# New orders for every engine's queue in a fused attention and MLP kernel

## The chip, the cores and the metric

The kernel runs on one core of a Trainium2 chip. The metric is the time of one execution on the device, in microseconds (us); of several runs the median is given.

## The reference

Eight batches with eight heads each attend over 16 beacon keys, which every query sees, and 576 causal keys. Then comes an MLP without bias, whose activation is the sigmoid form of GELU. All arrays are float32; the kernel computes in float16 and accumulates in float32.

```python
B, H, S, D = 8, 8, 576, 64              # 16 beacons
k_all = concatenate([beacon_k, k], axis=2); v_all = likewise
scores = q @ k_all.T / 8                # causal mask on the 576 keys only
a = exp(scores - max); a /= a.sum(-1)
x = (a @ v_all).transpose(0, 2, 1, 3).reshape(4608, 512)
h = x @ w_in                            # 512 x 2048
out = (h * sigmoid(1.702 * h)) @ w_out  # 2048 x 512
```

## The kernel before

**Attention.** The work is cut into 16 sets `s`; a set is one batch and four of its heads. A set's q and k are loaded with a cast to float16 (`ldqk`, on POOL's DMA queue) and turned by 32x32 transposes on VectorE (`turn`). The scores of a set come in chunks of 512 columns: TensorE computes a chunk (`qk`, L447), ScalarE takes the exponential into the tile `E` (`exp`, L458). There is one PSUM tile for scores, so the next `qk` waits for the `exp` before it. GpSimd masks the blocks on the diagonal in place (`mask`, L479). From set 4 on, VectorE adds the blocks of `E` up (`zadd`, L497). TensorE multiplies ones with these sums, and `E` with the values (`av`, L534; `av5.2.1` is the ones-product of set 5, half 1; `.0` and `.1` are the value products). VectorE transposes the sums, takes reciprocals and transposes back (`z1`, `z2`, L546 to L557), then scales the products into `xT` (`norm`, L569).

**MLP.** Tokens come in groups `g`: two of 256, then eight of 512. `m1` (L593) is the first product, sixteen pieces for a group of 512, with GELU behind it on ScalarE (`gelu`, L614; for the first two groups `tanh`, L607, and a `gate` on VectorE, L626). The second product of groups 2 to 9 uses seven products of half size in place of eight (a Strassen form): VectorE makes four sums of the activations (`s`, L658; four steps i that build on each other, for each of four slices), TensorE computes product p in four pieces (`m2.g.p.slice`, L707), and VectorE joins the products into four output tiles (`join`, L723; the first is copied by ScalarE, `half`, L718). SyncE's queue stores them (L730). The four output tiles `osb` come from a pool of four buffers, in turn. `u` is a ring of four PSUM banks, shared by `av`, `m1` and `m2`: a piece that opens a new tile in it waits until an older one was read.

**The order.** Nothing is scheduled automatically. All 1489 steps are made as `Op`s in a `Plan` (L117), in a fixed order of creation; the number of a step is its place there. The table `ORDER` (L16) lists, for each engine and for the DMA queue `Q`, the numbers in the order in which they are to run. `Plan.run` (L147) walks the lists with assumed durations and with the assumed delays `LAT` between engines, which gives each step a start. It sorts all steps by it to merge the lists into one program, and picks the bank of `u` for each tile by it. An engine's own sequence is its list, whatever the assumed times are. Waits between engines come from the reads and writes of the steps, through semaphores.

Some numbers that are used below, with what they stand for:

```
PE    414 qk19     221 m2.1.1.3 (last piece of group 1)   292..320 m1.2.*   1256 qk49
      352 m2.2.6.6   433 av4.1.1   474, 477 av5.2.*   480 av5.0.0   1115 av12.1.1
      972..1002 m1.6.*   1473 m2.9.4.6   1479 m2.9.5.6   1483..1486 m2.9.3.*
ACT   417, 415 exp of qk19   222 copy of m2.1.1   1257 exp of qk49
DVE   326, 327, 328 three s that build on each other   92 memset of beacon tiles
      353 join   473 zadd   1474, 1480, 1481, 1487 the last four joins
POOL  61 beacon values of batch 1   378 keys of set 4   396, 390 values of batch 2
      1076 values of batch 6   723 keys of set 9 (after turn 462)
SP    187, 217 stores of groups 0 and 1   93..96 beacon keys of sets 8 to 15
```

Of the kernel before, what the change touches and what calls it, by code (L numbers as in the profile page):

```python
# [17 lines left out]
        76, 100, 115, 118, 120, 106, 138, 141, 143, 108, 155, 111, 152, 129, 161, 158, 122, 131, 164, 167, 134, 127,  # L18
        170, 173, 176, 145, 125, 148, 150, 177, 182, 188, 191, 227, 194, 197, 232, 183, 203, 234, 200, 178, 237,
        179, 206, 258, 241, 209, 184, 263, 185, 212, 265, 213, 248, 246, 268, 214, 215, 401, 251, 253, 272, 218,  # L20
        404, 275, 244, 279, 219, 220, 407, 282, 284, 277, 221, 414, 320, 296, 304, 290, 302, 292, 300, 298, 312,
        308, 294, 318, 314, 310, 306, 316, 426, 435, 423, 343, 338, 339, 340, 433, 431, 438, 344, 345, 359, 349,
        341, 464, 346, 350, 351, 352, 354, 574, 355, 429, 360, 361, 577, 356, 362, 357, 372, 365, 583, 474, 477,
        373, 366, 374, 367, 605, 480, 484, 375, 482, 607, 368, 506, 502, 488, 492, 610, 490, 486, 498, 504, 500,
        508, 514, 510, 516, 494, 496, 512, 534, 593, 596, 535, 536, 539, 540, 550, 541, 542, 537, 742, 545, 546,
        547, 548, 603, 745, 551, 552, 553, 599, 601, 619, 622, 748, 555, 556, 557, 558, 561, 755, 625, 627, 629,
        562, 563, 776, 568, 564, 569, 570, 571, 779, 764, 767, 659, 637, 641, 657, 649, 651, 647, 661, 635, 631,
        653, 805, 772, 770, 774, 643, 655, 633, 639, 645, 679, 680, 815, 818, 700, 681, 682, 684, 701, 915, 690,
        685, 686, 691, 692, 702, 918, 687, 693, 695, 703, 696, 924, 821, 823, 697, 698, 706, 946, 825, 707, 713,
        708, 709, 948, 934, 937, 714, 715, 716, 827, 951, 944, 940, 942, 853, 831, 833, 855, 857, 851, 843, 835,  # L30
        837, 847, 839, 845, 829, 849, 841, 1083, 960, 963, 875, 876, 880, 877, 878, 881, 882, 1086, 968, 966, 970,
        883, 1089, 902, 909, 903, 886, 891, 1096, 887, 888, 889, 892, 893, 1117, 904, 894, 905, 896, 897, 1120, 898,
        899, 910, 911, 1105, 1108, 1146, 912, 976, 994, 996, 972, 978, 1000, 992, 982, 974, 998, 990, 984, 988, 980,
        1002, 986, 1256, 1156, 1113, 1111, 1115, 1159, 1025, 1020, 1026, 1021, 1259, 1022, 1027, 1031, 1023, 1028,
        1265, 1164, 1162, 1166, 1041, 1042, 1287, 1036, 1047, 1032, 1048, 1033, 1037, 1038, 1034, 1039, 1289, 1054,
        1055, 1049, 1056, 1043, 1044, 1050, 1292, 1057, 1198, 1172, 1168, 1178, 1184, 1180, 1194, 1170, 1174, 1176,
        1275, 1278, 1182, 1186, 1196, 1188, 1190, 1281, 1301, 1285, 1283, 1304, 1216, 1217, 1221, 1192, 1222, 1227,
        1218, 1223, 1228, 1219, 1224, 1232, 1229, 1233, 1230, 1307, 1311, 1309, 1237, 1327, 1333, 1238, 1243, 1234,
        1244, 1235, 1323, 1239, 1245, 1250, 1251, 1341, 1240, 1246, 1252, 1253, 1337, 1405, 1315, 1331, 1343, 1411,
        1335, 1321, 1403, 1431, 1313, 1325, 1407, 1419, 1317, 1423, 1425, 1319, 1339, 1421, 1409, 1329, 1361, 1413,  # L40
        1366, 1382, 1429, 1362, 1363, 1401, 1367, 1364, 1427, 1368, 1383, 1372, 1369, 1373, 1374, 1375, 1388, 1377,
        1389, 1378, 1390, 1395, 1379, 1384, 1380, 1385, 1391, 1396, 1415, 1397, 1398, 1470, 1454, 1417, 1455, 1449,
        1471, 1450, 1451, 1476, 1452, 1456, 1477, 1457, 1478, 1460, 1461, 1462, 1463, 1465, 1466, 1467, 1468, 1472,
        1479, 1473, 1483, 1484, 1485, 1486,
# [3 lines left out]
        195, 198, 233, 235, 201, 204, 238, 180, 207, 259, 210, 264, 186, 266, 269, 216, 402, 405, 408, 222, 417,  # L48
        415, 297, 291, 303, 305, 301, 299, 293, 309, 321, 295, 319, 313, 315, 311, 307, 317, 436, 439, 342, 465,
        468, 575, 578, 584, 587, 606, 608, 503, 507, 489, 491, 493, 487, 499, 505, 509, 515, 517, 495, 501, 511,  # L50
        497, 513, 611, 538, 743, 746, 749, 756, 758, 777, 780, 660, 642, 638, 652, 658, 648, 650, 636, 632, 662,
        654, 806, 644, 634, 656, 640, 646, 809, 916, 683, 919, 928, 925, 947, 949, 952, 828, 832, 854, 856, 852,
        858, 834, 838, 844, 840, 836, 846, 830, 848, 850, 842, 1084, 879, 1087, 1090, 1099, 1097, 1118, 1121, 1147,
        1150, 977, 995, 979, 997, 993, 973, 975, 983, 991, 999, 989, 1001, 981, 1003, 985, 987, 1257, 1260, 1024,
        1269, 1266, 1288, 1290, 1293, 1199, 1179, 1173, 1181, 1185, 1195, 1171, 1169, 1175, 1177, 1183, 1187, 1197,
        1189, 1191, 1193, 1220, 1328, 1334, 1324, 1342, 1316, 1332, 1344, 1406, 1412, 1338, 1336, 1404, 1432, 1314,
        1408, 1420, 1318, 1424, 1326, 1426, 1320, 1340, 1422, 1410, 1330, 1322, 1414, 1430, 1402, 1365, 1428, 1416,
        1418, 1453,
# [3 lines left out]
        123, 163, 160, 124, 224, 169, 128, 166, 172, 175, 146, 147, 126, 149, 151, 225, 226, 398, 190, 193, 196,  # L62
        199, 255, 256, 257, 202, 205, 286, 242, 411, 287, 211, 208, 243, 399, 249, 247, 400, 250, 412, 254, 252,
        273, 245, 274, 280, 276, 413, 281, 285, 283, 278, 289, 461, 288, 462, 419, 580, 420, 463, 326, 327, 328,
        421, 322, 92, 323, 324, 422, 427, 428, 424, 425, 325, 330, 334, 329, 335, 432, 336, 331, 434, 337, 332, 333,
        470, 347, 582, 353, 471, 581, 472, 430, 473, 358, 363, 475, 476, 478, 479, 481, 485, 739, 483, 369, 376,
        370, 589, 752, 740, 590, 615, 518, 753, 921, 519, 754, 526, 591, 527, 520, 528, 592, 529, 521, 741, 522,
        597, 523, 594, 530, 595, 598, 531, 802, 532, 524, 533, 616, 543, 525, 604, 549, 617, 618, 554, 600, 620,
        602, 623, 624, 621, 559, 760, 628, 761, 762, 626, 630, 565, 763, 566, 768, 572, 765, 811, 812, 766, 803,
        804, 769, 773, 771, 671, 1080, 775, 672, 813, 922, 663, 814, 664, 675, 667, 816, 673, 819, 668, 669, 817,  # L70
        923, 665, 666, 820, 674, 676, 677, 1093, 670, 688, 694, 678, 930, 822, 824, 699, 931, 826, 932, 933, 704,
        710, 938, 939, 935, 936, 717, 711, 945, 941, 943, 1081, 956, 957, 958, 871, 1082, 1094, 1095, 959, 872, 873,
        867, 859, 961, 962, 964, 965, 860, 863, 1262, 1143, 861, 874, 862, 868, 864, 967, 865, 971, 866, 969, 884,
        869, 870, 1101, 1144, 890, 1145, 1102, 895, 1103, 1104, 900, 906, 1109, 907, 1110, 913, 1106, 1107, 1152,
        1153, 1004, 1154, 1005, 1155, 1264, 1006, 1263, 1016, 1012, 1017, 1157, 1114, 1112, 1013, 1018, 1116, 1160,
        1008, 1161, 1009, 1019, 1158, 1014, 1015, 1029, 1010, 1165, 1011, 1007, 1163, 1167, 1035, 1040, 1271, 1051,
        1045, 1058, 1052, 1297, 1272, 1273, 1274, 1298, 1299, 1276, 1279, 1300, 1200, 1204, 1280, 1201, 1277, 1205,
        1282, 1302, 1206, 1286, 1284, 1208, 1305, 1209, 1202, 1303, 1210, 1212, 1203, 1306, 1207, 1213, 1225, 1231,
        1308, 1312, 1214, 1310, 1215, 1211, 1236, 1247, 1241, 1248, 1254, 1349, 1345, 1350, 1346, 1347, 1353, 1351,
        1354, 1355, 1356, 1357, 1358, 1359, 1370, 1348, 1360, 1352, 1376, 1381, 1386, 1392, 1393, 1445, 1446, 1433,  # L80
        1399, 1437, 1434, 1438, 1447, 1435, 1441, 1442, 1436, 1443, 1444, 1439, 1448, 1440, 1458, 1464, 1469, 1480,
        1474, 1481, 1487,
    ],
    "POOL": [
        8, 10, 12, 14, 16, 17, 19, 21, 23, 25, 27, 29, 31, 33, 35, 37, 39, 41, 43, 45, 47, 110, 49, 51, 113, 114,
        53, 55, 57, 59, 133, 61, 136, 137, 63, 65, 67, 69, 71, 378, 230, 231, 229, 380, 382, 384, 386, 236, 388,
# [29 lines left out]

class Plan:  # L117

    LANES = 8
    LAT = {"PE": 230, "ACT": 178, "DVE": 212, "POOL": 110, "Q": 1400, "SP": 0}

    def __init__(self, ring):
        self.ops = []
        self.ring = ring
        self.tiles = {}
        self.closers = {}
# [1004 lines left out]
```

## Time and profile before

| | us |
|---|---|
| median of 3 runs (329.2 to 330.05) | 329.88 |
| the profiled execution's own time | 328.92 |
| its span, first to last instruction | 327.2 |
| TensorE busy in the span | 314.6 |
| VectorE busy | 237.2 |
| ScalarE busy | 202.1 |
| GpSimd busy | 113.9 |

The granted clock of TensorE was 0.999 over the span. In stretches, from the trace (busy us of each engine):

| stretch, us | TensorE | VectorE | ScalarE | GpSimd |
|---|---|---|---|---|
| 0 to 30 | 22.25 | 18.30 | 17.90 | 21.60 |
| 30 to 62 | 31.66 | 26.73 | 21.83 | 19.10 |
| 62 to 101 | 38.31 | 32.23 | 29.56 | 16.27 |
| 101 to 164 | 63.00 | 55.74 | 46.89 | 26.12 |
| 164 to 213 | 49.00 | 42.57 | 35.84 | 24.29 |
| 213 to 245 | 32.00 | 20.32 | 21.87 | 4.27 |
| 245 to 285 | 40.00 | 20.75 | 16.57 | 2.28 |
| 285 to 327 | 38.38 | 20.57 | 11.62 | 0.00 |

A busy TensorE in this count is not TensorE at its peak: matmuls overlap, and a short wait between two of them can be hidden in the modelled end of the first. So the lengths of pieces are taken below from one start to the next.

### The profile page before, as it was taken

To read this page: it belongs to the slowest core of one execution; us is meant where nothing else is said; L and a number is where in the kernel's file an instruction comes from. 1 tells how busy PE (TensorE), PEld (TensorE's weight loads), DVE (VectorE), ACT (ScalarE), POOL (GpSimd) and SP (SyncE) were. 2 spreads that over 40 slices of the span, in tenths; PEclk is the share of its full clock that TensorE was granted. 3 is DMA by queue.
4 is the path that set the end of the run, shared out by engine and by line. 5 is a ranking of instruction groups with operands and counts; after the bars stand their busy time and mean duration, and the time that the engine had idled before them with its cause. 6 is when DMAs were issued, how large, how long until landed. Compare 5 with 4: busy or idle time off the path is not lost.

```text
span 327.2 us, 9966 instructions
## 1 busy us (share of the span) xinstructions
PE 314.6 (96%) x4364; PEld 214.7 (66%) x4364; DVE 237.2 (72%) x480; ACT 202.1 (62%) x236; POOL 113.9 (35%) x178
## 2 busy tenths in 40 slices
PE   6589999999999999999999999999999999999995
PEld 6467665545775477746878878547764776447884
DVE  4838798777987989977998798858558853006674
ACT  1676697678767586679666786868577212674010
POOL 8765478190419312941177019400042000000000
PEclk9999999999999999999999999999999999999999
DMA  7999999293424911792039709500120012000122
GB/s 126 159 201 211 204 186 184 37 123 107 99 72 64 190 34 34 79 198 43 7 53 178 119 4 124 154 2 3 34 98 0 2 34 83 15 0 2 65 98 97
DMA packets 58220, 28.83 MB, mean 88 GB/s; under 512 B 41280, under 2 KB 53568, under 8 KB 58176
## 3 DMA queue, kind: packets, MB, share of 16 engines
q0 software_dynamic: 47552, 18.49, 47.9%
q1 hardware_dynamic: 10560, 9.69, 9.2%
q8 instruction: 34, 0.56, 0.7%
q14 instruction: 10, 0.08, 0.1%
q10 hardware_dynamic: 64, 0.01, 0.0%
HBM read 37.22 MB, written 9.44 MB: 143 GB/s over the span
## 4 chain that ended last, share of the span: by engine, by line
PE 83%; DMA 6%; DVE 4%; POOL 3%; ACT 2%; issue 1%; ACTq 0%; POOLq 0%
PE u L593 34%; PE u L707 30%; PE u L534 9%; PE s L447 7%; PE u L638 3%; DMA w<-in_moe_w_out_dram 3%; DMA w<-in_moe_w_in_dram 3%; ACT E L458 1%; DVE sA L658 1%; DVE g L626 1%; POOL vb L378 1%; POOL w L384 0%; DVE bkn L403 0%; ACT L614 0%; DVE kT L418 0%
## 5 line engine op out<-in xcount | busy, mean ns | idle before, releaser
L593 PE MATMUL u<-xT,w 128*128 128x512 f16 (+1 forms) x704 | 130.6, 341 | 0.6 <-ACT g L614 0.5
L458 ACT ACTIVATE E<-s 128x2048 f16<-128x2048 f32 (+5 forms) x66 | 98.9, 1515 | 44.9 <-PE s L447 44.4
L614 ACT ACTIVATE g<-u 128x512 f16<-128x512 f32 x128 | 70.5, 598 | 53.7 <-PE u L593 53.2
L593 PEld LDWEIGHTS <-w 128*128 128x128 f16 x704 | 67.6, 98 | 54.3 <-issue 1.9
L479 POOL TENSOR_SCALAR_AFFINE_SELECT E<-E 128x512 f16<-128x512 f16 (+3 forms) x78 | 49.3, 665 | 110.8 <-ACT E L458 79.1
L723 DVE SCALAR_TENSOR_TENSOR osb<-u,osb 128x512 f32<-128x512 f32 x56 | 37.3, 683 | 24.5 <-PE u L707 22.5
L707 PEld LDWEIGHTS <-g 128*128 128x128 f16 x512 | 48.3, 98 | 9.3 <-issue 0.2
L707 PE MATMUL u<-w,g 128*128 128x256 f16 x384 | 50.6, 273 | 0.0
L447 PE MATMUL s<-qT,kT 32*128 32x32 f16 (+20 forms) x1376 | 34.6, 228 | 5.7 <-ACT E L458 2.8
L447 PEld LDWEIGHTS <-kT 32*128 32x128 f16 x1376 | 25.2, 92 | 22.5 <-issue 14.4
L707 PEld LDWEIGHTS <-sA 128*128 128x128 f16 x384 | 36.3, 98 | 5.3 <-issue 0.3
L707 PE MATMUL u<-tB,sA 128*128 128x256 f16 x256 | 35.1, 273 | 0.1
L658 DVE TENSOR_TENSOR sA<-g 128x512 f16<-128x512 f16 x32 | 12.9, 416 | 26.2 <-ACT g L614 26.2
L569 DVE TENSOR_TENSOR xT<-u,rz 128x352 f16<-128x352 f32 (+2 forms) x52 | 25.5, 517 | 6.5 <-PE u L534 6.3
L378 POOL DMA_DIRECT2D vb<-in_v_dram x32 | 27.4, 876 | 2.4 <-DMA qn<-in_q_dram 1.6
L534 PE MATMUL u<-E,vb 128*32 128x352 f16 (+8 forms) x928 | 27.4, 262 | 0.0
L497 DVE TENSOR_TENSOR zs<-zs,E 128x1344 f16<-128x1344 f16 (+2 forms) x36 | 22.7, 633 | 5.3 <-POOL E L479 4.4
L534 PEld LDWEIGHTS <-vb 128*32 128x32 f16 (+1 forms) x928 | 19.9, 96 | 5.5 <-issue 1.7
L418 DVE STREAM_TRANSPOSE kT<-kn 128x576 f32<-128x576 f32 x16 | 20.1, 1257 | 2.1 <-DMA kn<-in_k_dram 1.4
L418 DVE STREAM_TRANSPOSE qT<-qn 128x576 f32<-128x576 f32 x16 | 19.9, 1241 | 0.3 <-DMA qn<-in_q_dram 0.3
L546 DVE STREAM_TRANSPOSE zt<-u 128x224 f32<-128x224 f32 (+2 forms) x32 | 15.0, 470 | 5.9 <-PE u L534 5.8
L497 DVE TENSOR_TENSOR zs<-E 128x1856 f16<-128x1856 f16 x12 | 15.8, 1320 | 3.3 <-POOL E L479 3.3
(48 smaller groups left out, 252.3 us busy)
## 6 DMA issues: line engine op xcount, KB each, us to landing
out_dram<-osb SPq DMA_DIRECT2D x36, 256.0 KB, 2.4
kn<-in_k_dram POOLq DMA_DIRECT2D x16, 288.0 KB, 6.9
qn<-in_q_dram POOLq DMA_DIRECT2D x16, 288.0 KB, 6.5
vb<-in_v_dram POOLq DMA_DIRECT2D x24, 128.0 KB, 6.4
w<-in_moe_w_in_dram POOLq DMA_DIRECT2D x8, 256.0 KB, 9.4
w<-in_moe_w_out_dram POOLq DMA_DIRECT2D x4, 512.0 KB, 13.5
vb<-in_v_dram POOLq DMA_DIRECT2D x8, 112.0 KB, 5.0
vb<-in_v_dram POOLq DMA_DIRECT2D x8, 80.0 KB, 7.9
```

What stands on the lines that cost most here:

```text
L378: nc.gpsimd.dma_start(out=t[0 : hi - lo, j, h0:h1, :], in_=v[b, h0:h1, lo:hi, :].rearrange("h n d -> n h d"),)
L418: nc.vector.transpose(out=f32(dst.rearrange("p n e -> p (n e)")).rearrange("p (r t) -> p t r", t=TR), in_=f32(src[:, :]).rearrange("p (t c ...
L447: nc.tensor.matmul(sc[:, h, o : o + w], kT[s % NB2][r : r + 32, j * P : (j + 1) * P, d], qT[s % NB2][r : r + 32, a : a + w, d], start=(d = ...
L458: nc.scalar.activation(out=Es[s][:, :, c0:c1], in_=ss[i][:, :, o : o + c1 - c0], func=AFT.Exp, scale=0.125,)
L479: nc.gpsimd.affine_select(out=blk, in_=blk, compare_op=ALU.is_ge, fill=0.0, base=off + (Nb if j == 0 else 0), pattern=[[0, Q], [1, w]], ch ...
L497: nc.vector.tensor_tensor(out=t, in0=E[:, :, Z0:S] if i == 1 else t, in1=E[:, :, wcol[i] : wcol[i] + S - a], op=ALU.add,)
L534: nc.tensor.matmul(u[32 * h : 32 * h + 32, a:e], lhs, src[0:kw, h, col : col + e - a], start=first, stop=last,)
L569: nc.vector.tensor_tensor(out=xT[:, 2 * hs + x : 2 * hs + x + n, t0 : t0 + w], in0=rings[("av", s, x, half)][:, 0 : n * w].rearrange("p (n ...
L593: nc.tensor.matmul(u[:, o + a - t0 : o + e - t0], w1t[:, kp, nt * P : (nt + 1) * P], xT[:, kp, a % XR : (e - 1) % XR + 1], start=(kp == 0) ...
L614: nc.scalar.activation(out=gts[g][:, n0:n1, 0:w], in_=rings[("m1", g, n0)][:, 0 : n * w].rearrange("p (n w) -> p n w", n=n), func=AFT.Gelu ...
L707: nc.tensor.matmul(u[:, HM * mt : HM * (mt + 1)], lhs[:, n, mt * P : (mt + 1) * P], rhs[:, n, :], start=(n == 0 and mt == 0), stop=(n == H ...
L723: nc.vector.scalar_tensor_tensor(out=osbs[(g, dst)][:, :], in0=rings[("p", g, p)][:, :], scalar=scale_of(g), in1=osbs[(g, src)][:, :], op0 ...
```

## The change

The lists in `ORDER` are replaced; each holds the same numbers as before. PE's first differs at its 22nd entry (409 of 523 places differ), ScalarE's at the 29th (141 of 224), VectorE's at the 26th (350 of 425), POOL's at the 32nd (132 of 171), SP's at the 16th (10 of 54). `LAT["SP"]` goes from 0 to 2200, and `products` gets dependences in the plan: a step that writes an output tile depends on the store that last read that buffer. No instruction is added to or taken from the program by hand.

```diff
 "PE":
-        170, 173, 176, 145, 125, 148, 150, 177, 182, 188, 191, 227, 194, 197, 232, 183, 203, 234, 200, 178, 237,
+        173, 176, 127, 145, 125, 148, 150, 177, 182, 188, 191, 227, 194, 197, 232, 183, 203, 234, 200, 178, 237,
...
-        404, 275, 244, 279, 219, 220, 407, 282, 284, 277, 221, 414, 320, 296, 304, 290, 302, 292, 300, 298, 312,
+        404, 246, 277, 279, 275, 219, 407, 282, 284, 220, 414, 221, 292, 296, 298, 300, 294, 302, 290, 304, 316,
...
+        899, 910, 911, 912, 1146, 1108, 1105, 978, 994, 982, 992, 988, 974, 972, 990, 984, 980, 1256, 1111, 1115,
+        1159, 1113, 1156, 986, 996, 976, 998, 1002, 1000, 1020, 1259, 1021, 1025, 1022, 1047, 1026, 1027, 1031,
...
-        1479, 1473, 1483, 1484, 1485, 1486,
+        1478, 1473, 1479, 1483, 1484, 1485, 1486,
 "ACT":
+        1147, 979, 983, 995, 993, 975, 973, 991, 985, 989, 981, 1257, 987, 997, 977, 1003, 999, 1001, 1260, 1266,
...
 "DVE":
-        328, 421, 322, 92, 323, 324, 422, 427, 428, 424, 425, 325, 330, 334, 329, 335, 432, 336, 331, 434, 337, 332, 333,
+        257, 199, 256, 202, 286, 411, 398, 205, 242, 208, 400, 287, 211, 399, 249, 412, 243, 245, 250, 254, 461,
+        323, 327, 324, 328, 334, 427, 424, 425, 428, 330, 335, 325, 329, 434, 336, 331, 580, 332, 333, 337, 470,
...
-        1474, 1481, 1487,
+        1474, 1480, 1481, 1487,
 "POOL":
-        53, 55, 57, 59, 133, 61, 136, 137, 63, 65, 67, 69, 71, 378, 230, 231, 229, 380, 382, 384, 386, 236, 388,
+        53, 55, 57, 59, 133, 378, 136, 137, 396, 63, 65, 71, 67, 380, 229, 231, 236, 230, 443, 61, 382, 69, 384,
+        721, 723, 455, 390, 437, 440, 453, 418, 466, 451, 719, 725, 467, 576, 579, 585, 588, 737, 782, 469, 609,
+        1091, 1119, 1127, 1131, 1151, 1148, 1100, 1076, 1135, 1122, 1137, 1149, 1258, 1261, 1267, 1268, 1291, 1295,
...
 "SP":
-        0, 2, 4, 5, 6, 7, 83, 84, 85, 86, 88, 89, 90, 91, 181, 93, 94, 95, 96, 187, 217, 223, 348, 364, 371, 377,
+        0, 2, 4, 5, 6, 7, 83, 84, 85, 86, 88, 89, 90, 91, 181, 187, 217, 94, 93, 96, 95, 223, 348, 364, 371, 377,
...
-    LAT = {"PE": 230, "ACT": 178, "DVE": 212, "POOL": 110, "Q": 1400, "SP": 0}
+    LAT = {"PE": 230, "ACT": 178, "DVE": 212, "POOL": 110, "Q": 1400, "SP": 2200}
...
-    tanhs, gated = [], []
+    tanhs, gated, outs = [], [], []
...
+        was = outs[-4:]
+
         def store(o, i, r, c):
-            op("SP", 60, [o], lambda: e_store4(g, i, r, c), name="store")
+            outs.append(op("SP", 60, [o], lambda: e_store4(g, i, r, c), name="store"))
 
         prod(1)
-        half = op("ACT", 480, [last[1], ends.get(g - 1)], lambda: e_half(g, 1, "m"), pr=1, closes=("p", g, 1), name="half")
+        half = op("ACT", 480, [last[1], ends.get(g - 1), was[0]], lambda: e_half(g, 1, "m"), pr=1, closes=("p", g, 1), name="half")
         prod(2)
-        c11 = join(2, "m", "a", [half])
+        c11 = join(2, "m", "a", [half, was[1]])
...
-        u3 = join(7, "m", "u", [u2])
+        u3 = join(7, "m", "u", [u2, was[2]])
         prod(4)
-        c21 = join(4, "u", "b", [u3])
+        c21 = join(4, "u", "b", [u3, was[3]])
...
         ends[g] = c12
+        outs[-4:] = outs[-1:] + [outs[-4], outs[-2], outs[-3]]
...
-            op("SP", 60, [ev], lambda g=g, mt=mt: e_store(g, mt), name="store")
+            outs.append(op("SP", 60, [ev], lambda g=g, mt=mt: e_store(g, mt), name="store"))
```

## The prediction

> **What bounds the kernel now.** I read the page's engine rows, the table by stretches, TensorE's waits, then its timeline.
>
> ```profile
> span 327.2 us, 9966 instructions
> ...
> PE 314.6 (96%) x4364; PEld 214.7 (66%) x4364; DVE 237.2 (72%) x480; ACT 202.1 (62%) x236; POOL 113.9 (35%) x178
> ...
> PE   6589999999999999999999999999999999999995
> ...
> PE 83%; DMA 6%; DVE 4%; POOL 3%; ACT 2%; issue 1%; ACTq 0%; POOLq 0%
> ```
>
> TensorE is the bound: its busy slices are full from the fifth to the last but one, and it holds 83% of the chain that ended last. No matmul is added or removed. So a new order can change two things only: what TensorE pays between pieces, and how long it waits. From the second score product of set 1 (`av1.2.1`, 30.16 us) to the start of the last piece (322.78) lie 292.6 us. The pieces' own lengths, as the code's plan has them, plus the cost of the switches below, sum to 289.8 (with no switch between two pieces, start to start differs from the plan's length by 0.004 us on average, over 305 pairs after 70 us). So about 2.8 us are waits: 0.7 of it by 61.9 us, 1.2 from there to 101.3, 0.9 in the 222 us behind.
>
> TensorE's timeline shows both kinds:
>
> ```profile
> 64.83 0.64 PE L447 MATMUL s<-qT,kT 32*128 32x384 f16 x24
> 65.40 3.63 PE L593 MATMUL u<-xT,w 128*128 128x512 f16 x16
> 69.52 10.52 PE L593 MATMUL u<-xT,w 128*128 128x512 f16 x48 [0.49 <-ACT g L614]
> ...
> 94.28 0.60 PE L707 MATMUL u<-w,g 128*128 128x256 f16 x4
> 94.72 0.60 PE L707 MATMUL u<-w,sA 128*128 128x256 f16 x4
> 95.15 0.60 PE L707 MATMUL u<-tB,sA 128*128 128x256 f16 x4
> 95.69 0.66 PE L447 MATMUL s<-qT,kT 32*128 32x208 f16 x40
> ```
>
> The first three rows are a wait: four pieces fill the ring of banks, the fifth must wait for the first GELU. In the last four, pieces of the same kind follow each other in 0.43 to 0.44 us; ahead of the `qk` it is 0.54: changing the shape of the array cost 0.10.
>
> **1. Switches of TensorE's shape.** Taken as above over the trace after 70 us, by the kinds before and after (r `qk`, c `av`, m `m1` and `m2`), one switch costs: m to r 0.10, r to m 0.12, c to m 0.105, m to c 0.095, r to c 0.12, c to r 0.11. Counted in the two lists, 149 become 143: c to m 26 to 20, r to c 21 to 16, m to r 44 to 43, r to m 33 to 38, c to r 10 to 11. Sum: -0.63 - 0.60 - 0.10 + 0.60 + 0.11 = -0.6 us, all on TensorE. Bounds by the dearest and cheapest switch: six times 0.095 to 0.12, -0.6 to -0.7.
>
> **2. The wait at 69.5 us.** ScalarE's rows there:
>
> ```profile
> 64.93 0.60 ACT L651 ACTIVATE osb<-u 128x512 f32<-128x512 f32 x1 [0.38 <-PE u L638]
> 65.62 1.94 ACT L458 ACTIVATE E<-s 128x1536 f16<-128x1536 f32 x2
> 67.58 1.28 ACT L614 ACT_TABLE_LOAD   x1
> 68.87 1.08 ACT L614 ACTIVATE g<-u 128x512 f16<-128x512 f32 x2
> ```
>
> Before, the first GELU ends 69.47 - 64.83 = 4.64 after `qk19` starts; TensorE has 0.57 + 4 x 0.864 = 4.03 of work: 0.6 waited. Now 221 (0.86) comes behind `qk19`, so TensorE has 5.0 with a switch, but the copy 222 comes between the two exponentials and ends later, so the GELU ends at 5.4. About 0.4 is waited: -0.2. Before that, three `norm`s must come ahead of 292: `av3.2.1` ends near 60.0, then `z1`, a turn (1.24), the memset (0.48), `z2` (0.7) and three norms (0.45 each) end near 63.9, ahead of 65.3. No new wait.
>
> **3. VectorE between 72 and 101 us.** Neighbours where the second reads the first's result start later:
>
> ```profile
> 74.91 0.40 DVE L658 TENSOR_TENSOR sA<-g 128x512 f16<-128x512 f16 x1
> 75.35 0.42 DVE L658 TENSOR_TENSOR sA<-sA,g 128x512 f16<-128x512 f16 x1
> 75.81 0.42 DVE L658 TENSOR_TENSOR sA<-g,sA 128x512 f16<-128x512 f16 x1
> 76.15 0.58 DVE L497 TENSOR_TENSOR zs<-zs,E 128x832 f16<-128x832 f16 x1
> ```
>
> 326 to 327 to 328 take 0.44 and 0.46; 328 to an independent `zadd` 0.34. Over the trace an independent step starts 0.08 before its neighbour's end (310 pairs), a dependent one 0.03 behind it (53 pairs). Such pairs go from 63 to 50: 13 x 0.116 = 1.5 us less of VectorE, worth something only where TensorE waits for it. That is here: at 80 to 86 us it waits for `z1`, `z2` and `s` in turn. I take 0.3 of the 1.2 us lost between 62 and 101, bounds 0 and 1.0 (the rest of it). What is late next are the ones-products of set 5: they come 2.0 us behind the end of 352 (before 4.5), with a join (0.68) and a `zadd` (0.30) between. With 0.3 for the handings over that is 1.3. It fits if VectorE has no backlog. With the overlap of 0.08 in its twenty-odd steps from 79.7 it ends in time; without it, TensorE would wait 0.7. I keep that as a bound.
>
> [...]
>
> **4. Other short distances.** In TensorE's time, from the end of the last piece that feeds it, with the work between: 1.39 ahead of m1.5.9 and 1.66 ahead of m1.3.11 (a `norm` of 0.52, 0.8 with the handings over); 1.31 ahead of m2.8.2.2 and m2.9.1.6 (a GELU of 0.60, 0.8 likewise); `qk19` comes 2.64 behind `qk18`, and `qk24` (92.81, 0.65 long, its exponential 93.53 to 95.41) shows the least possible as 2.64. All just fit: 0; if not, 0.1 to 0.5 each.
>
> **5. Two more table loads.** Exponential 1257 now lies among the GELUs of group 6: 2 x 1.28 us of ScalarE. By hand: the last GELU ahead of it ends 0.7 behind `qk49`'s issue, load, 1.88, load: the next GELU, 987, can start 5.1 behind and ends at 5.7. The ring first needs it for 1002, 5.8 behind (2.3 us of `qk49` and `av`, then four pieces of 0.86): 0, with 0.1 to spare; uncovered, up to 2.6.
>
> **6. POOL and its loads.** The 78 masks and the loads now alternate; POOL has 35% of work. A load holds POOL 0.55 to 0.9 and the masks behind it as long. The loads that come nearest to their use: 390 is behind 723, which waits for turn 462; issued near 74.5 it has 7.6 us until 433. 1076, behind masks of set 13, has 5.7 until 1115. The time to landing:
>
> ```profile
> kn<-in_k_dram POOLq DMA_DIRECT2D x16, 288.0 KB, 6.9
> ...
> vb<-in_v_dram POOLq DMA_DIRECT2D x24, 128.0 KB, 6.4
> ```
>
> That median is over bursts; in the stretch 63 to 70 us such a load landed in 3.8, in 196 to 201 in 4.3, in the burst at 172 to 176 in 10.2. The new list issues few at a time, so I take 4.3: 0. Bounds 0 and 10.2 - 5.7 = +4.5. 396 comes early and waits for `av1.1.1` (32.5): behind it queue 63, 65, 71 and 67, not needed before 52, and a mask whose exponential ends at 38.7. 0.
>
> **7. Merge, buffers, SP, end.** The new dependences and `LAT` shift assumed starts only, so they emit nothing; another bank may be picked, and a bank that is really freed later could cost 0.1 to 0.6, as in part 2. SP: 187 and 217 pass ahead of the loads 93 to 96, which wait for memset 92, now earlier too; the buffers are next written from 87.4, the beacon tiles read from 100: 0. At the end the last four pieces are the same; 1474 now goes ahead of 1480, and the three joins, before one run of 2.02 us to 323.25, again end just ahead of 1487 at 323.4: 0, at most 0.1.
>
> **Sum.** -0.6 - 0.2 - 0.3 = -1.1. Span 327.2 to 326.1; own time 328.92 - 1.1 = 327.8. The profiled execution ran 0.96 below the median of the three, so the median becomes 329.88 - 1.1 = 328.8. About 0.3% (1.0 us) is what a measurement of this kernel can tell from no change.
>
> **Rivals.**
> - *The waits move (329.8).* TensorE saves the 0.6, but the ring or VectorE is late elsewhere: parts 3 and 4 hold a bound of 0.7 and of 0.1 to 0.5. For it: VectorE and ScalarE are 72% and 62% busy, and the distances of part 4 were 8 to 14 us before, `qk19`'s apart; against: VectorE gets lighter. With +0.5 it nets -0.1. Part of this is that the change does not do what it says, if lighter neighbours are not where TensorE waits.
> - *Slower: a load lands late (331.9).* 1076 or 390 lands as in the burst at 104 to 110 us (8.2): 2.5 us of wait at 1115, with only -0.5 saved: +2.0. It decides beyond a landing of 5.7 + 1.1 + 1.0 = 7.8. For it: median 6.4 and maximum 11.3 of these loads; against: few are queued ahead of it.
> - *All of part 3's wait goes (328.1):* -0.6 - 0.2 - 1.0 = -1.8.
>
> The Trainium skill, "SBUF — State Buffer", section "SBUF: two separate sides", says that VectorE with two SBUF inputs and a GpSimd operation that reads SBUF exclude each other, so masks spread among more `s` could slow both. A row here goes with it (an `s` of 0.80 at 85.03, elsewhere 0.42, beside a mask), but POOL's time is no term above.
>
> **How the numbers follow.** Forecast 0.37; all of part 3's wait goes 0.08: faster 0.45. Waits move 0.33: same. A load or many small waits 0.22: slower. Alone, the forecast reaches from 328.1 to 328.9. The range takes in -1.8 and a little of the 0.9 behind 101 us: 327.5, and of the slower cases those to +1.6: 331.5. Left out: 0.05 below, 0.12 above.
>
> **What would show it.** Right: 143 switches at the same price; the wait for a GELU near 69 us at 0.4; TensorE's row without new waits behind 101 us; two more table loads, one pair near 214 to 218 us with no gap behind them. Wrong: TensorE waiting for values ahead of `av12.1.1` or `av4.1.1`, for a join ahead of `av5.2`, or for a bank near 58, 130 or 170 us; a longer total with the same TensorE sum.

## The result and the profile after

The changed kernel takes 331.94 us (median of 6 runs, 331.36 to 332.64), the kernel before 329.54 beside it (6 runs, 328.56 to 330.05). The ratio is 1.0088, 95% interval 1.0073 to 1.0104: 2.4 us slower. The forecast was 328.8 with a range up to 331.5. The profiled execution after took 332.32, its span is 330.6.

From the page of the kernel after (a line of the source has its number of before plus 3 where it lies behind the edit in `products`; the lines named here have the same number in both):

```profile
span 330.6 us, 9955 instructions
...
PE 318.0 (96%) x4364; PEld 216.0 (65%) x4364; DVE 238.2 (72%) x480; ACT 203.0 (61%) x238; POOL 117.5 (36%) x178
...
PE   7699999999999999999999999999999999999995
...
PEclk9879999999999999999999999999999999999999
...
PE 77%; DMA 7%; ACT 5%; POOL 4%; DVE 3%; issue 2%; ACTq 0%; DVEq 0%; POOLq 0%
```

TensorE is still the bound, but its share of the chain fell from 83% to 77%. ScalarE has two more instructions, the two table loads of part 5. The granted clock dips in the first 30 us of this one execution; two other executions of the same kernel had a clock of 1.000 and spans of 329.7 and 330.9, so the dip is not the cause. VectorE was to get lighter, and is 1.0 busier.

TensorE's waits from 31 us on, first before, then after (us in total, times, longest):

```profile
PE u L593 <- ACT g L614: 0.5, 1, 0.5
```

```profile
PE u L707 <- DVE g L658: 1.2, 2, 0.8
PE s L447 <- DVE kT L418: 0.4, 1, 0.4
PE u L534 <- DVE xT L569: 0.4, 1, 0.4
PE u L593 <- ACT g L614: 0.2, 1, 0.2
```

The wait for GELU got shorter, and three new kinds came, all for VectorE. (Short waits are hidden here in the modelled ends.) Counted as in the prediction (a piece's start, less the lengths and switches ahead of it, from `av1.2.1`, the ones-product of set 1's second half, to the last piece):

| | before | after |
|---|---|---|
| `av1.2.1` starts | 30.16 | 31.37 |
| lengths and switches behind it | 289.80 | 289.20 |
| waits, sum | 2.81 | 5.58 |
| of it: `qk8` (37.8), for k of set 2 | 0 | 0.49 |
| the first GELU of group 2 (70) | 0.66 | 0.28 |
| `av5.2.1` (95.3), for a bank that a `norm` frees | 0 | 0.61 |
| `m2.4.7.6` (168.0), for `s` 678 | 0 | 0.58 |
| `m2.5.7.6` (204.3), for `s` 874 | 0 | 0.89 |
| fifth piece of group 6 (`m1.6.4`, 214.2; before `m1.6.9`, 210.9), for the first GELU behind a table load | 0.16 | 0.28 |
| last piece starts | 322.78 | 326.16 |

3.4 us are 1.2 of start, -0.6 of switches and 2.8 of waits; 2.1 of the waits lie in the three places at 95, 168 and 204 us. What the table leaves out is small; the largest is a wait for GELU at 153 us, 0.32 (before 0.15). The medians differ by 2.4 only: the profiled execution lies 0.6 below its median before, and 0.4 above it after.

What is in front of the dearest of them is seen in VectorE's, POOL's and TensorE's timelines of the kernel after:

```profile
201.33 1.11 DVE L497 TENSOR_TENSOR zs<-E 128x1856 f16<-128x1856 f16 x1
202.36 1.86 DVE L658 TENSOR_TENSOR g<-g 128x512 f16<-128x512 f16 x1
204.15 0.68 DVE L723 SCALAR_TENSOR_TENSOR osb<-u,osb 128x512 f32<-128x512 f32 x1
```

```profile
201.34 2.61 POOL L479 TENSOR_SCALAR_AFFINE_SELECT E<-E 128x320 f16<-128x320 f16 x3
```

```profile
202.81 0.65 PE L447 MATMUL s<-qT,kT 32*128 32x320 f16 x24
204.28 0.61 PE L707 MATMUL u<-w,g 128*128 128x256 f16 x4 [0.82 <-DVE g L658]
```

An `s` of 512 columns is 0.42 us nearly everywhere. This one starts as a `zadd` ends, while three masks run one behind the other, and takes 1.86: it ends 0.3 behind the last mask. TensorE waits for just this tile. At 168 us an `s` of 0.85 lies beside a mask in the same way:

```profile
167.07 0.85 DVE L658 TENSOR_TENSOR g<-g 128x512 f16<-128x512 f16 x1
```

```profile
165.97 1.68 POOL L479 TENSOR_SCALAR_AFFINE_SELECT E<-E 128x320 f16<-128x320 f16 x2 [2.46 <-ACT E L458]
```

At 95 us it is a `zadd`:

```profile
93.36 0.68 DVE L723 SCALAR_TENSOR_TENSOR osb<-u,osb 128x512 f32<-128x512 f32 x1
93.96 0.74 DVE L497 TENSOR_TENSOR zs<-zs,E 128x320 f16<-128x320 f16 x1
94.63 0.61 DVE L569 TENSOR_TENSOR xT<-u,rz 128x448 f16<-128x448 f32 x1
```

```profile
93.37 1.16 POOL L479 TENSOR_SCALAR_AFFINE_SELECT E<-E 128x320 f16<-128x320 f16 x2
```

```profile
94.64 0.23 PE L534 MATMUL u<-E,ones 128*32 128x80 f16 x8
95.29 0.33 PE L534 MATMUL u<-zs,ones 128*32 128x352 f16 x4 [0.43 <-DVE xT L569]
```

The short `zadd` took 0.29 before, here 0.74 beside a mask; the `norm` behind it frees the bank late.

### The profile page after: what moved, and what is told of

Its sections match the earlier page's. It is cut to its first block, busy times and chain, and to the rows that moved or that the text cites. A ratio compares the mean times of both kernels' runs of the same rounds, so it can differ in the third digit from the quotient of the medians.

```text
span 330.6 us, 9955 instructions
## 1 busy us (share of the span) xinstructions
PE 318.0 (96%) x4364; PEld 216.0 (65%) x4364; DVE 238.2 (72%) x480; ACT 203.0 (61%) x238; POOL 117.5 (36%) x178
## 4 chain that ended last, share of the span: by engine, by line
PE 77%; DMA 7%; ACT 5%; POOL 4%; DVE 3%; issue 2%; ACTq 0%; DVEq 0%; POOLq 0%
PE u L593 32%; PE u L707 27%; PE u L534 8%; PE s L447 7%; DMA qn<-in_q_dram 4%; ACT E L458 3%; PE u L638 3%; DMA w<-in_moe_w_in_dram 3%; POOL vb L378 1%; ACT L614 1%; DVE g L658 1%; POOL E L479 1%; POOL w L384 1%; ACT g L614 1%; DVE osb L723 0%
## 5 line engine op out<-in xcount | busy, mean ns | idle before, releaser
L614 ACT ACTIVATE g<-u 128x512 f16<-128x512 f32 x128 | 69.6, 598 | 48.6 <-PE u L593 48.0
L479 POOL TENSOR_SCALAR_AFFINE_SELECT E<-E 128x512 f16<-128x512 f16 (+2 forms) x78 | 53.1, 696 | 89.1 <-ACT E L458 81.4
L707 PE MATMUL u<-tB,sA 128*128 128x256 f16 x256 | 35.9, 273 | 0.0
L534 PE MATMUL u<-E,vb 128*32 128x352 f16 (+8 forms) x928 | 28.4, 266 | 0.9 <-DMA vb<-in_v_dram 0.9
L497 DVE TENSOR_TENSOR zs<-zs,E 128x1344 f16<-128x1344 f16 (+2 forms) x36 | 24.2, 672 | 4.5 <-POOL E L479 3.7
L707 PE MATMUL u<-tB,g 128*128 128x256 f16 x128 | 18.8, 273 | 0.0
```

Source lines behind the costliest of these rows:

```text
L479: nc.gpsimd.affine_select(out=blk, in_=blk, compare_op=ALU.is_ge, fill=0.0, base=off + (Nb if j == 0 else 0), pattern=[[0, Q], [1, w]], ch ...
L497: nc.vector.tensor_tensor(out=t, in0=E[:, :, Z0:S] if i == 1 else t, in1=E[:, :, wcol[i] : wcol[i] + S - a], op=ALU.add,)
L534: nc.tensor.matmul(u[32 * h : 32 * h + 32, a:e], lhs, src[0:kw, h, col : col + e - a], start=first, stop=last,)
L614: nc.scalar.activation(out=gts[g][:, n0:n1, 0:w], in_=rings[("m1", g, n0)][:, 0 : n * w].rearrange("p (n w) -> p n w", n=n), func=AFT.Gelu ...
L707: nc.tensor.matmul(u[:, HM * mt : HM * (mt + 1)], lhs[:, n, mt * P : (mt + 1) * P], rhs[:, n, :], start=(n == 0 and mt == 0), stop=(n == H ...
```

## The experiments

Two theories on the three waits. *M*: the new orders of POOL and VectorE put masks beside VectorE steps that TensorE waits for next, and a mask holds such a step. *P*: those steps simply stand too far back in VectorE's list. The first two runs were made on a plainer one, that POOL's list as a whole is to blame (the expectations of runs 1 to 4 have letters of their own). Each was timed beside the kernel before on the same chip, whose median was 329.08 to 329.16 us each time.

| run | median, us | ratio to before, 95% |
|---|---|---|
| after, again | 331.67 | 1.0077 (1.0063 to 1.0091) |
| 1 after, POOL's list of before | 333.91 | 1.0151 (1.0133 to 1.0168) |
| 2 before, POOL's list of after | 328.90 | 0.9995 (0.9987 to 1.0004) |
| 3 after, two `s` earlier | 330.48 | 1.0040 (1.0027 to 1.0053) |
| 4 after, turn of k first | 331.16 | 1.0064 (1.0051 to 1.0077) |
| 5 after, masks elsewhere | 330.94 | 1.0051 (1.0038 to 1.0064) |
| 6 after, no masks | 329.47 | 1.0009 (1.0000 to 1.0017) |
| 7 before, no masks | 328.51 | 0.9978 (0.9969 to 0.9987) |
| 8 after, `av0.1.1` as before | 331.62 | 1.0079 (1.0066 to 1.0092) |
| 9 after, mended | 329.52 | 1.0017 (1.0008 to 1.0026) |
| 10 mended, from 127 us as before | 329.26 | 1.0007 (0.9998 to 1.0016) |
| 11 the same, first 36 us as before too | 329.24 | 1.0002 (0.9994 to 1.0011) |

**Runs 1 and 2: POOL's list alone.** The first takes the changed kernel with POOL's (and the DMA queue's) list of before up to about 184 us, the second the kernel before with the changed list up to 137 us.

```diff
 # run 1
-"POOL", "Q": the changed lists
+"POOL", "Q": those of before up to POOL's entry 143, then the changed order
 # run 2
-"POOL", "Q": the lists of before
+"POOL", "Q": the changed ones up to POOL's entry 114, then the order of before
```

> The changed kernel, with GpSimd's list (and its DMA queue's) as before up to the loads of set 14 (entry 143, some 180 us) and as changed behind it. Theory C (masks and two-input VectorE steps hold each other up, and the changed GpSimd list puts them beside each other): the waits of TensorE near 95 and 168 us shrink, the one near 204 us (0.9) stays; 0.5 to 1.2 us faster than the changed kernel (331.9 to 330.7-331.4). Theory L (the lists of TensorE and VectorE are too tight by themselves): no change, 331.6 to 332.2.

> The kernel before, with GpSimd's list and its DMA queue's as changed up to entry 114 (some 140 us) and as before behind it. Theory C: new waits of TensorE where a mask meets an s or a zadd, 0.3 to 1.0 us slower than before. Theory L: no change within 0.3 us.

Both speak against POOL's list as the cause: 2.0 us more instead of less, and no difference. In run 1 new waits came where VectorE's list expects a mask early (1.59 us at 92.3). The waits at 168 and 204 us stayed (0.56 and 0.80): there too three masks ran one behind the other beside the two `s`, which took 0.80 and 1.28. So the other changed lists need POOL's changed one, while the order of before runs with either.

**Run 3: the two `s` earlier on VectorE**, ahead of the `zadd`s and a turn (and a load between two masks near 93 us).

```diff
 "DVE":
-    674, 930, 931, 678, 694,  ...  969, 1145, 1101, 874, 890,
+    674, 678, 930, 931, 694,  ...  969, 874, 1145, 1101, 890,
 "POOL":
-    451, 719, 725, 467, 576,
+    451, 725, 467, 719, 576,
```

> The changed kernel with two s steps of VectorE moved ahead (874 to behind 969, 678 to behind 674) and a load of GpSimd (719) put between the masks 467 and 576, so that the steps that TensorE waited for near 95, 168 and 204 us no longer run beside a mask. If these three waits (0.61, 0.58, 0.89) are on the path to the end: 1.5 to 2.0 us faster than the changed kernel, near 330.0. If what is saved there is lost at the next short distance: under 0.6 us faster.

The waits at 168 and 204 us are gone, and the time falls by 1.2 to 1.5 us, from 331.7 or 331.9 to 330.48 (1.5 to 2.0 were expected, with the wait at 95 us gone too). VectorE's and POOL's timelines of this run:

```profile
199.83 0.41 DVE L651 TENSOR_TENSOR g<-g 128x512 f16<-128x512 f16 x1
...
201.26 1.45 DVE L490 TENSOR_TENSOR zs<-E 128x1856 f16<-128x1856 f16 x1
```

```profile
201.22 2.57 POOL L472 TENSOR_SCALAR_AFFINE_SELECT E<-E 128x320 f16<-128x320 f16 x3
```

(In this source the numbers of the lines are 7 lower.) The three masks are where they were; the `s` is 0.41 again, and what stands beside them is a `zadd` (1.45 in place of 1.11) behind which TensorE shows no wait. The edit changed place and neighbour at once, so it does not tell *M* from *P*. The wait at 95 us stayed (0.62): the `zadd` now met the next mask.

**Run 4: the turn of k first.** Before, VectorE turned k of set 2, then q; the changed order has q first, which waits 0.50 us for its load, with k behind it.

```diff
 "DVE":
-    149, 226, 225, 190,
+    149, 225, 226, 190,
```

> The changed kernel with the turns of set 2 in the order of before (k, 225, ahead of q, 226). Theory D (q lands last, and the k turn behind it then delays qk8, by 0.49 in the profile): TensorE's wait ahead of qk8 goes, 0.3 to 0.5 us faster than the changed kernel, 331.5. Rival (the wait there only takes the place of the one for the exponential at qk9): 0 to 0.1 us.

The wait ahead of `qk8` is gone and the median 0.5 to 0.8 lower. In the profiled execution 0.48 us appear inside `m2.1.1.2` at 64 us, where TensorE waited for nothing that the profile shows.

**The changed kernel again, and runs 5 to 7: are the masks the cause?** Run 5 edits POOL's list alone: loads change places with the masks beside the three steps. Runs 6 and 7 leave out GpSimd's masks (VectorE's few stay) and keep every list; what they compute is not the reference's result.

```diff
 # run 5, "POOL":
-    466, 451, 719, 725, 467, 576, 579, ... 927, 926, 1125, 1064, 792, ... 1098, 1092, 1091, 1119, 1127, 1131,
+    466, 467, 451, 719, 725, 579, 576, ... 927, 1125, 1064, 926, 792, ... 1098, 1127, 1131, 1092, 1091, 1119,
 # runs 6 (after) and 7 (before), in the step that masks
+        if eng != "DVE":
+            return
```

> The changed kernel once more, unedited. In its first profile TensorE waited 5.6 us between the second score product of set 1 and the last piece (2.8 before), 2.1 of it in three places: 0.61 at 95 us, 0.58 at 168 us, 0.89 at 204 us. Theory M (VectorE steps with two inputs in SBUF are held by GpSimd's masks, because the order puts them beside each other): the three places come again, each within 0.2 us, since the order is fixed. Rival R (an accident of that execution, its clock of 0.99 with it): one of them is missing or differs by more than 0.3 us, and the three change by over 0.6 in sum. Time 331.5 to 332.4 by both.

> Only POOL's list is edited: loads are put where the masks were that lay beside the zadd ahead of av5.2.1 (95 us), the s ahead of m2.4.7.6 (168 us) and the s ahead of m2.5.7.6 (204 us); VectorE's list stays the changed one to the entry. Theory M (the masks hold those steps): they take 0.30, 0.42 and 0.42 us again in place of 0.74, 0.85 and 1.86, the three waits of 0.61 + 0.58 + 0.89 = 2.1 us go, and the time is 331.9 - 2.1 = 329.8 (ratio to before 1.001 to 1.004). Rival P (the steps lie too far back in VectorE's list, whatever GpSimd does): the waits stay above 1.5 us in sum and the time at 331.3 or more. Rival N (they go and as much comes back where the moved masks and loads are now): the three go, the time stays above 331.

> The changed kernel without the causal masks that GpSimd applies (VectorE's masks stay), so its output is not the reference's; every list stays, GpSimd keeps its loads. Theory M: nothing is left that holds the two-input steps of VectorE; no s takes over 0.6 us, the waits of 95, 168 and 204 us are gone, and the time is 328.8 to 330.0. Rival P (place in VectorE's list, or the table loads and the ring): at least 1.5 of the 2.1 us stay, time 331 or more.

> The kernel before without GpSimd's causal masks, edited in the same way (output not the reference's). Theory M: before had few masks where TensorE waited next, so it gains little, 0 to 0.6 us: 328.6 to 329.5, and the changed kernel without masks stands 0.3 to 1.0 above or below it, in place of 2.4 to 2.8 above. Rival P: it gains as much as the changed one does, and the difference between the two stays 2 us or more.

The three waits came again to the hundredth (0.61, 0.58, 0.89). In run 5 the one at 204 us is gone, with VectorE's list untouched: the `s` 874 took 0.85 in place of 1.86. The `zadd` at 95 us is back to 0.30, and its wait went from 0.61 to 0.40; a turn, 581, stands ahead of it too, which may be the rest. The `s` at 168 us still took 0.85 and its wait stayed, though no mask is recorded beside its first half. So this run shows *M* for one place and part of another and leaves the rest open; the time fell by 0.7, not 2.1.

Run 6 decides the larger part. VectorE's groups by shape, after and in run 6, where the numbers of the lines are 5 lower (count, then busy us and mean ns):

```profile
L658 DVE TENSOR_TENSOR g<-g 128x512 f16<-128x512 f16 x32 | 15.6, 506 | 0.0
L497 DVE TENSOR_TENSOR zs<-E 128x1856 f16<-128x1856 f16 x12 | 15.3, 1283 | 3.5 <-POOL E L479 2.6 <-ACT E L458 0.9
```

```profile
L653 DVE TENSOR_TENSOR g<-g 128x512 f16<-128x512 f16 x32 | 12.7, 414 | 0.0
L492 DVE TENSOR_TENSOR zs<-E 128x1856 f16<-128x1856 f16 x12 | 13.3, 1112 | 0.7 <-ACT E L451 0.4
```

Without masks every `s` takes 0.43 or less, the waits at 95, 168 and 204 us are gone with the lists unchanged, and the changed kernel gains 2.2 us (331.67 to 329.47); before gains 0.6 (329.14 to 328.51). The gap shrinks from 2.5 to 1.0. So the masks make 1.6 of the 2.5 us, and place in the list without them (*P*) does not make the three waits. Without masks VectorE's plain waits for a mask's result go as well; but the `zadd`s had 7.7 us of these before and 6.3 after, so they do not explain why the changed kernel gains more. In what stays, the wait ahead of `qk8` is the largest that run 6 shows against before (0.74).

**Run 8: one TensorE piece back in its place.** `m2.0.0.0` reads weights that land at 29 to 30 us. Before, `av0.1.1` (0.6 long) ran ahead of it.

```diff
 "PE":
-    134, 170, 173, 176, 127, 145,
+    134, 127, 170, 173, 176, 145,
```

> The changed kernel with one piece put back on TensorE: av0.1.1 (127) ahead of m1.0.12, m1.0.14 and m2.0.0.0, as before, in place of behind them. m2.0.0.0 reads the first half of the output weights, which land at 29 to 30 us. In the profiles with the changed order it waits 0.5 to 0.9 us for them (before 0 to 0.3). Theory W (the piece filled that time): the wait falls to 0 to 0.3 us, av1.2.1 starts about 0.6 earlier relative to qk7, and the time is 331.7 to 331.4 (after's two medians 331.94 and 331.67, less 0.3 to 0.6): 331.1 to 331.5, ratio 1.006 to 1.007. Rival F (the start is only noise of the first loads): no change, 331.7 to 331.9, with the wait now ahead of another piece.

The wait of `m2.0.0.0` fell and `av1.2.1` starts at 30.20 us, but then it waits in its middle for a mask, which stands behind a load ahead of which POOL idles 1.6 us: the piece behind it starts at 31.46, against 31.61 in the changed kernel's second profile. The time is 331.62, no gain: the wait only moved (rival *F* in effect).

**Run 9: all of it mended at once.** The edits of runs 3 (VectorE), 4, 5 and 8, and:

```diff
 "DVE":
-    472, 581, 353, 473, 430, 478,
+    472, 473, 353, 430, 581, 478,
```

> The changed kernel with all the causes found taken away at once: av0.1.1 ahead of m1.0.12 (TensorE), turn k ahead of turn q for the beacon of set 2, the s 874 and 678 ahead of the zadds, the zadd 473, join 353 and norm 430 ahead of turn 581 (VectorE), and POOL's masks away from them. If these four explain the loss, the sum is 331.8 - 0.5 (weights) - 0.5 (turn, ahead of qk8) - 0.6 (95 us) - 1.5 (168 and 204 us) = 328.7, ratio to before 0.997 to 1.000, and TensorE's waits from av1.2.1 on are 2.5 to 3.0 us in place of 5.5. If they are symptoms of a VectorE that is late in general, the waits come back at other places and the time stays above 330.

329.52, 0.4 above the kernel before: 2.1 of the 2.5 us are back. The waits in its profile are 3.05 us; those at 37, 95, 168 and 204 us are gone, one of 0.31 is new at 94 us, and the only waits from 31 us on that the profile puts down to another engine are for GELU (line numbers 7 lower again):

```profile
PE u L586 <- ACT g L607: 0.4, 2, 0.2
```

The median is 0.8 above what was expected, and the profiled execution (329.05) is the lowest of 12 (up to 330.59).

**Runs 10 and 11: can the good part be kept?** At piece 619 (97 us behind `av1.2.1`) the mended kernel is 0.92 us ahead of before, at the end only 0.28. Both runs go over to the order of before at that piece.

```diff
 # run 10: every list
-the mended order
+the mended order up to 126.7 us, then the order of before
 # run 11
+the order of before up to 36 us, the mended one up to 126.7 us, the order of before
```

> The lists of the mended kernel up to 126.7 us and, behind that, the order of before. In the two profiles, counted from the start of av1.2.1, the mended kernel is 0.92 us ahead of before at the piece 619 (96.2 against 97.1 us), and only 0.28 at the last piece: behind 127 us the changed order loses 0.6. If stages add up, this splice keeps the lead: 0.9 us less than before from av1.2.1 on, TensorE's waits 1.9 to 2.2 us, time 328.2 to 328.6 (ratio 0.997 to 0.999). If the start of the changed order is itself 0.4 later, as the mended kernel's median hints, it is 328.6 to 329.0. If the order of before behind the seam finds its inputs late: 329.3 or more.

> As the last, and also the order of before in the first 36 us: so only the stretch from 36 to 127 us has the changed, mended order. If the changed start costs time (0.3 to 0.6 us, which the profiles of it suggest but scatter about), this one is that much faster than the last: 328.0 to 328.4. If the start only scatters from execution to execution, the two agree within 0.3 us.

Neither beats before. In run 10's profile the lead at the seam is only 0.17. In run 11's it is 0.56 there and 0.05 from 4 us later on: three waits of 0.18, 0.19 and 0.20 just behind the seam take it. The two runs agree to 0.02 us, so the other engines' changed lists in the first 36 us show no steady cost. `av1.2.1` does start later with the changed start of TensorE's list (30.4 to 31.8 over seven profiles, 30.2 to 30.5 over the other seven), so the 1.2 us in the table are not only that execution; but run 8, which takes the later start away, gains nothing.

## Why the prediction was wrong, point by point

- **Part 1, right.** 149 to 143 switches: -0.6 predicted, 289.80 to 289.20 counted. The prices hold: read from the trace after in the same way, a switch costs 0.09 to 0.12 us there too.
- **Part 2, right in mechanism.** -0.2 predicted; the wait went from 0.66 to 0.28, -0.4. ScalarE's rows show the copy between the two exponentials, as foreseen, and the first GELU ends 5.1 behind `qk19`, not 5.4:

```profile
66.30 1.45 ACT L458 ACTIVATE E<-s 128x1536 f16<-128x1536 f32 x1 [0.84 <-PE s L447]
67.65 0.59 ACT L651 ACTIVATE osb<-u 128x512 f32<-128x512 f32 x1
68.13 0.60 ACT L458 ACTIVATE E<-s 128x512 f16<-128x512 f32 x1
68.75 1.28 ACT L614 ACT_TABLE_LOAD   x1
70.05 1.09 ACT L614 ACTIVATE g<-u 128x512 f16<-128x512 f32 x2
```

- **Part 3, the step that failed.** -0.3 was taken for waits between 62 and 101 us, from a lighter VectorE. Behind the GELU wait the loss there was 0.46 before and 0.66 after. The bound that the prediction set aside came true at the place it named: 0.7 said "ahead of `av5.2`", 0.61 measured ahead of `av5.2.1`. The reason was another one. That bound was for a VectorE without the overlap of 0.08 us, and the overlap is there in the trace after; with the same lists and no masks (run 6) the wait at 95 us is gone.
- **The same failure where nothing was looked at.** The prediction quoted an `s` of 0.80 beside a mask, and said: "POOL's time is no term above". That sentence left out the largest term: by runs 6 and 7 the masks make 1.6 of the 2.5 us. The masks cost VectorE 238.2 - 228.4 = 9.8 us after and 237.2 - 228.9 = 8.3 us before (busy time with and without them). The rise of 1.5 is as much as the 13 pairs of part 3 were to save. Most of the toll is harmless; but with masks TensorE waits 0.58 and 0.89 us for an `s` ahead of `m2.4.7.6` and `m2.5.7.6`, behind 101 us, where parts 4 to 7 summed to 0, and without masks it waits there for neither.
- **Part 4, right for the places it named** (no wait over 0.12 us at any of them), but its list of short distances was not complete: `s` 678 and 874 were not on it, nor the turn of k ahead of `qk8` (0.49).
- **Part 5, right but for a size.** "0, with 0.1 to spare" ahead of 1002; measured 0.12 there. GELU 987 starts 5.3 behind `qk49`, not 5.1. The 0.28 at `m1.6.4` comes from another load, ahead of the group's first GELU, which before has too (0.16).
- **Part 6, right for the loads it named.** Behind 31 us TensorE waited for no load itself (but VectorE waited 0.50 for q of set 2, and the wait of 0.49 ahead of `qk8` came of it); loads landed sooner than before:

```profile
kn<-in_k_dram POOLq DMA_DIRECT2D x16, 288.0 KB, 5.4
...
vb<-in_v_dram POOLq DMA_DIRECT2D x24, 128.0 KB, 4.4
```

The rival "a load lands late" gave 331.9, the measured time, by luck: its mechanism did not occur.
- **Part 7, right.** Given the lists of before, the changed dependences and `LAT` produce the same instructions on every engine; all of the loss is in the lists.
- **Rival "the waits move"** came nearest: VectorE late elsewhere, with +0.5 for what measured +2.8. It had no masks in it.
- **The price of dependent neighbours, right.** In the trace after, too, an independent neighbour starts 0.08 us before the end (314 pairs), a dependent one 0.02 behind it (46 pairs). The Trainium skill, "VectorE: DVE Perf Modes", section "The DRAIN you can't avoid", has the next operation wait until the pipe is empty, and adds that one which is not held (made to wait for those ahead of it) starts earlier; the rows go with that. What the 13 pairs were to save does not show in TensorE's waits, which grew.

What stays open: what held the `s` at 168 us in run 5, which begins beside two loads and has a mask beside it only from 0.5 us on; in run 6 seventeen `s` beside loads took 0.43 at most. And run 9's median is about 0.5 above its profiled execution; no second profile of it was taken.

## What to carry to other kernels

Before a new order is priced, list for each engine the steps that the bound engine waits for next, and look at what GpSimd will run beside each step of VectorE among them, not only at VectorE's own queue. A total of busy time says little: the masks' toll rose by 1.5 us in 238, and where it fell made most of the loss (1.6 of 2.5). A list exchanged alone can bring waits of its own (run 1), so take a suspected cause away (here the masks) rather than exchange one list.

## What the runs showed of the hardware

- A mask on GpSimd slows just some VectorE steps. In the trace after, alone and overlapping a mask by over 0.1 us (median us, count): `s` 0.42 (117) and 0.69 (11, longest 1.86); `norm` 0.52 (41) and 0.52 (11); `join` 0.68 (47) and 0.68 (9); `gate` 0.68 (10) and 0.68 (6). The first reads two tiles of SBUF, the other three read one operand from PSUM. Lying beside a mask is not enough: in the trace before, twelve `s` overlapped one, with a median of 0.42 and 0.85 at most.
- The Trainium skill, "SBUF — State Buffer", section "SBUF: two separate sides", states this: VectorE with two SBUF inputs and a GpSimd operation that reads SBUF exclude each other for a whole instruction. The runs agree, in both directions: at 201.33 the `zadd` kept its 1.11 us, and of the three masks that began with it the first took 1.43, the others 0.63 each.
- Not expected: an `s` that comes while masks stand in a row waits for more than the one that runs. 1.86 - 0.42 = 1.44 us is over two masks of 0.63.
